# A dynamic convolution fused with a max-out layer: another order for the opening's steps, and a last copy split over two engines

## The chip, the core and the metric

The kernel runs on one core of a Trainium2 chip. The metric is the device time of one execution in microseconds. Five engines work side by side, each through its own list of instructions in order: TensorE (PE, matrix products; PEld is its weight load), VectorE (DVE), ScalarE (ACT), GpSimd (POOL) and SyncE (SP, here only an issuer of transfers). Transfers issued by SP form one queue ("hardware" in the profile), those issued by POOL another ("software"); both are moved by the same 16 DMA engines. Engines wait for each other and for transfers through semaphores.

## The reference, cut to what matters

```python
# x: (8, 4160, 192), weight_gen: (8, 4160, 8 heads, 7 taps), all float32
w = exp(weight_gen - max); w = w / w.sum(taps)        # softmax over the 7 taps
out = sum over k of w[..., h, k] * x[s - 6 + k, h*24:(h+1)*24]   # causal, zero before the sequence
x2 = out.reshape(33280, 192)
h1 = x2 @ w1; h2 = x2 @ w2                            # 192 -> 1024
return maximum(h1, h2) @ w_out                        # 1024 -> 192
```

## The kernel before, in words

The 33280 rows lie as 128 partitions of 260 columns; a column is one row of 192 numbers in each partition. Columns are handled in batches of 16 (`BATCHES`), each in two units of 8, in the first two batches in four units of 4. For a batch the softmax is worked out on ACT and DVE: exp (`exp_sum`, L153), sum over taps on DVE (`red`, L168), logarithm on ACT (`ln`, L172), subtraction on DVE (`shift`, L177), and a second exp that writes normalised weights in bfloat16 (`weights`, L191). DVE multiplies them with the seven shifted copies of x (`mul`, L211). From batch 2 on DVE also adds the seven products and a DMA transposes the sum; in the first two batches PE adds and transposes with an identity (`sum_transpose`, L281) and ACT copies the result out of PSUM (`sums_out`, L293).

The maximum is written as max(h1, h2) = h1 + relu(h2 - h1). So PE computes the hidden tile x2 @ (w2 - w1) (`hid_tile`, L336), ACT applies relu (L346), and PE adds rows of x2 @ (w1 @ w_out) (`out_first`, L388) and relu(...) @ w_out (`out_hidden`, L376) into an output bank, in a first half (`out_first`) and a second half (`out_second`); between them ACT relays a semaphore (`relay`). ACT copies the bank to SBUF (`evac`, L434) and SP stores it.

The work up to hidden tile 15 is the opening, the rest is a loop over groups of three tiles that the change does not touch. In the opening the order is written out by hand: the string `OPENING` is a list of steps, and as each step is run its instructions are appended to the lists of their engines. So the string sets the order on every engine at once. `step@other` makes a transfer wait until `other` is done. The steps, with their numbers:

- `lg.b` loads weight_gen of batch b (SP for b < 2, POOL after that). `xf` loads the first columns of x by SP, `lx.b.o.n` n columns of batch b from column o by POOL, which turns them into bfloat16 on the way. `xa`, `xv` convert the first columns on ACT and DVE.
- `lw.h.i` loads 512 columns (half h) of rows 0 to 127 of w1 (i = 0) or w2 (i = 1); `lt.h.i` the same half of the last 64 rows, into 64 partitions. All by SP. `lo` loads w_out by POOL.
- `X`, `n`, `l`, `s`, `W.b.o`: the five softmax steps. X.0, n.0, l.0 and s.0 come in halves (`.0.0.2`, `.0.1.2`). `m.b.o` is the product, `y.u` the sum on PE of unit u, `e.u` its copy on ACT (unit 0 in two halves, y.0.0 and y.0.1).
- `c.i` casts a piece of w1 (L622, ACT); `d.i` is w2 - w1 on DVE (L597); `t.i` exchanges its partition halves on PE, `T.i` copies that back on ACT (L614, L616).
- `v`, `V`: w1 transposed on PE and copied on ACT; `p`: w1 @ w_out on PE, `C.i` its three copies on ACT (L665, L667). `lh` copies the six columns that two batches share.
- `h.t`, `r.t`: hidden tile t on PE and its relu on ACT. `A.g`, `B.g`, `D.g`, `E.g`: first half, relay, second half and copy of output group g.
- `k.n` issues n matmuls on the identity that nobody reads.

Hidden tiles of the opening lie in two PSUM buffers, so h.8 can start only when r.6 has read tile 6. `evac` treats the last pair of columns apart (L422 to L425).

Of the kernel before, what the change touches and what calls it, by code (L numbers as in the profile page):

```python
# [17 lines left out]
def _sub(base: bass.AP, off: int, dims):  # L18
    ap = [list(base.ap[0])] + [[int(s), int(c)] for s, c in dims]
    return dataclasses.replace(base, offset=base.offset + off, ap=ap)  # L20
# [3 lines left out]
def kernel(  # L24
# [9 lines left out]
    nc = tc.nc  # L34

    B, S, D = x.shape
# [17 lines left out]
    def dcol(c):  # L54

        return (c + ROT) % CPP
# [292 lines left out]
    def column(c):  # L349

        for u, (b, o, n) in enumerate(UNITS):
            k = c - BATCHES[b][0] - o
            if 0 <= k < n:
                return u, k // 2, k % 2

    def place(p):

        u, i, _ = column(2 * p)
        b, o, n = UNITS[u]
        return BATCHES[b][0] + o + i, n // 2  # L360
# [55 lines left out]
    def evac(p, n):  # L416

        tile_, at = op_at[p]
        o = o_t[0]
        if p == NT // 2 - 1:  # L420

            nc.scalar.copy(out=_sub(o_last, 0, [[D, 2], [1, D]]),  # L422
                           in_=_sub(tile_, at, [[512, 2], [1, D]]))
            for j, eng in enumerate((nc.scalar, nc.sync)):
                eng.dma_start(  # L425
                    out=bass.AP(tensor=out.tensor, offset=dcol(place(p)[0] + 2 * j) * D, ap=[[CPP * D, P], [1, D]]),
                    in_=o_last[:, j * D:(j + 1) * D],
                )
            return
        runs = [[q for q in range(p, p + n) if column(2 * q)[0] == u]  # L430
                for u in range(column(2 * p)[0], column(2 * (p + n - 1))[0] + 1)]
        for qs in runs:
            c, h = place(qs[0])
            copied = nc.scalar.copy(out=_sub(o, c % 24 * D, [[D, len(qs)], [h * D, 2], [1, D]]),  # L434
                           in_=_sub(tile_, at + (qs[0] - p) * D, [[D, len(qs)], [512, 2], [1, D]]))
        stores = []
        for q in range(p, p + n):
            u, i, _ = column(2 * q)
            if u == NU - 2 and UNITS[u][2] == 8 and i % 2:
                stores.append((nc.sync, place(q)[0] - 1, [4 * D, 2], [1, 2 * D]))  # L440
            elif u < NU - 1 and i == UNITS[u][2] // 2 - 1:
                w = i + 1
                for k in range(0, 2 * w, w if u in PARTED else 2 * w):
                    stores.append((nc.sync, place(q)[0] - i + k, [1, (w if u in PARTED else 2 * w) * D]))
            if u == NU - 1:
                stores.append((nc.sync, place(q)[0], [2 * D, 2], [1, D]))
        for eng, c, *ap in stores:

            def issue(eng=eng, c=c, ap=ap, o=o):
                eng.dma_start(  # L450
                    out=bass.AP(tensor=out.tensor, offset=dcol(c) * D, ap=[[CPP * D, P], *ap]),
                    in_=_sub(o, c % 24 * D, ap),
                )

            if 3 <= u < NU - 3:
                held.append(issue)
            else:
                while u > 3 and held:
                    held.pop(0)()
                issue()  # L460
        return copied
# [8 lines left out]
    OUTS, c = [[], [], []], 0  # L470
    for g in range(3, len(GROUPS)):
        most = 4 if g == 3 else 2 if GROUPS[g][1] == 2 or len(OUTS[-1]) == 4 else 4
        n = min(most, ready[g] - c)
# [21 lines left out]
    def hidden(g, now=(), between=lambda: None, beside=lambda: None, ahead=lambda: None,  # L495
               before=lambda: None, after=lambda: None):


        t0, n = GROUPS[g]
        rd = room(g)  # L500
        for t in range(t0, t0 + n - 1):
            hid_tile(t)
        if now:
            out_room(now, "a" if n == 1 and "a" in ps else None)
            last = out_first(now)
        for t in range(t0, t0 + n - 1):
            relu(rd, t, 1)
        go = relay(last) if now else None
        hid_tile(t0 + n - 1)
        before()  # L510
        if len(now) > 2:
            beside()
        relu(rd, t0 + n - 1, 1)
        ahead()
        if now:
            out_second(now, go)
            evac(now[0] // 2, len(now) // 2)
        between()
        after()
        if len(now) <= 2:  # L520
            beside()

    def rest_of_results(c):

        parts = [p for p in (c[:4], c[4:-2], c[-2:]) if p]
        assert max(map(len, parts)) <= 4
        go = []
        for i, now in enumerate(parts):
            out_room(now, ("r", "a", "c")[i])
            go.append(relay(out_first(now)))  # L530
            if i:
                out_second(parts[i - 1], go[i - 1])
                evac(parts[i - 1][0] // 2, len(parts[i - 1]) // 2)
        out_second(parts[-1], go[-1])
        evac(parts[-1][0] // 2, len(parts[-1]) // 2)
# [10 lines left out]
    o_last = consts.tile([P, 2 * D], FP32, name="o_last")  # L546
# [155 lines left out]
    def results_buffer(_):  # L702
# [16 lines left out]
    }  # L719

    OPENING = """
        lg.0 xf.-6.6 xf.0.4 lt.1.0 lt.0.0 k.2 lw.0.1 k.19 lw.0.0 lt.1.1 lw.1.0 lt.0.1 X.0.0.2 k.1 n.0.0.2
        X.0.1.2 lw.1.1 k.1 k.2 n.0.1.2 l.0.0.2 s.0.0.2 xa.-6.4 l.0.1.2 W.0.0.0 lx.0.4.4@l.0.0.2 lg.1 xv.-2.6
        W.0.0.1 s.0.1.2 W.0.12 c.0 lx.0.12.4@W.0.12 W.0.8 m.0.0.0 m.0.0.1 W.0.4 y.0.0 y.0.1 c.2 e.0.0 c.1
        e.0.1 d.0 d.2 t.0 k.3 t.2 T.3 d.1 T.4 h.0 h.1 t.1 X.1 r.0 lx.0.8.4 T.1 lo.0 r.1 m.0.4 n.1 v.0 h.2
        lx.1.0.8 V.1 y.1 r.2 l.1 h.3 e.1 m.0.8 lg.2@l.1 s.1 V.0 m.0.12 r.3 h.4 W.1.0 m.1.0 y.2 h.5 r.4 p.0
        e.2 r.5 h.6 lx.1.8.8@r.4 lg.3@e.2 y.3 W.1.8 h.7 lh.2 C.1 C.0 C.2 A.3 W.1.4 X.2 r.6 e.3 B.3 m.1.4 h.8
        D.3 y.4 r.7 r.8 Z.0 E.3 n.2 X.3 l.2 m.1.8 A.4 e.4 W.1.12 lx.2.0.8.0@r.7 B.4 h.9 D.4 h.10 r.9 E.4 s.2
        r.10 lg.4@r.9 y.5 W.2.0 A.5 h.11 B.5 h.12 e.5 D.5 n.3 r.11 r.12 A.6 m.1.12 E.5 h.13 B.6 D.6 y.6 r.13
        E.6 h.14 e.6 l.3 lx.2.8.8@r.13 h.15 r.14 A.7 W.2.8 B.7 y.7 D.7 r.15 e.7 E.7  # L730
    """

    make_identity(nc, ident_f)
# [91 lines left out]
```

## Time and profile before

| | us |
|---|---|
| median of three runs | 405.75 (405.36 to 405.82) |
| profiled execution | 405.37 |
| span of its core | 403.6 |
| PE busy | 394.8 |
| DVE busy | 369.1 |
| ACT busy | 360.9 |
| POOL busy | 72.3 |

The span runs from the first to the last recorded instruction; 1.77 us of the profiled execution lie around it. Times in the views count from the span's start. A row of the timeline gives start, duration, engine, line, operation, tiles and count, and in brackets the idle time before it with what ended it; rows of the same kind that follow each other are merged. The granted clock of TensorE was 1.0 throughout.

### The profile page before, as it was taken

The numbers are of one execution on the slowest core, as the hardware profiler recorded it, in microseconds if no ns is written. First come the engines' busy times: TensorE is split into PE (matmuls) and PEld (weight loads), VectorE is DVE, ScalarE is ACT, GpSimd is POOL, SyncE is SP. The second block draws the span as 40 slices with busy tenths as digits, with TensorE's granted clock in tenths as the row PEclk, the third lists the DMA queues.
The fourth block names the chain that finished last, engine by engine and source line by source line (L and its number), as shares of the span: only waits on it lengthen the run. The fifth ranks groups of instructions, "written<-read, shape, count | busy, mean of one in ns | idle before, by whom it ended". The sixth has DMA issues, their size and how long they took to land.

```text
span 403.6 us, 16321 instructions
## 1 busy us (share of the span) xinstructions
PE 394.8 (98%) x7499; PEld 321.3 (80%) x7499; DVE 369.1 (91%) x211; ACT 360.9 (89%) x466; POOL 72.3 (18%) x96
## 2 busy tenths in 40 slices
PE   7799999999999999999999999999999999999996
PEld 3589999777778777778777778877777877787996
DVE  5999999999999999999999999999999999998200
ACT  5999899999999989999899999989999899888872
POOL 3111031211122210222220122122012121200000
PEclk9999999999999999999999999999999999999999
DMA  8956468767768646864766667777457847558304
GB/s 262 222 140 151 120 124 167 183 164 133 190 110 222 182 79 129 240 187 80 217 187 107 141 192 193 99 215 198 81 115 228 178 80 200 141 106 193 104 31 169
DMA packets 60883, 63.16 MB, mean 157 GB/s; under 512 B 47641, under 2 KB 48665, under 8 KB 60816
## 3 DMA queue, kind: packets, MB, share of 16 engines
q1 hardware_dynamic: 52816, 40.15, 36.4%
q0 software_dynamic: 7856, 21.89, 27.4%
q8 instruction: 58, 0.95, 1.0%
q10 hardware_dynamic: 144, 0.10, 0.1%
q14 instruction: 9, 0.07, 0.1%
HBM read 36.55 MB, written 25.56 MB: 154 GB/s over the span
## 4 chain that ended last, share of the span: by engine, by line
PE 92%; ACT 5%; DMA 1%; SPq 1%; issue 0%
PE op_ps L376 42%; PE hdc L336 13%; PE hdb L336 13%; PE hda L336 13%; PE op_ps L388 8%; ACT rd_t L346 2%; DMA ws0E<-in_moe_w_dram 1%; PE hdp L336 1%; PE yps L281 1%; ACT en_t L191 1%; ACT yt L293 1%; ACT e_t L153 0%; ACT w1t L644 0%; SPq L574 0%; ACT w L622 0%
## 5 line engine op out<-in xcount | busy, mean ns | idle before, releaser
L376 PE MATMUL op_ps<-wo,rd_t 64*128 64x192 bf16 x4160 | 210.6, 243 | 0.0
L376 PEld LDWEIGHTS <-rd_t 64*128 64x128 bf16 x4160 | 181.0, 94 | 14.7
L211 DVE TENSOR_TENSOR m_t<-xb,en_t 128x10752 bf16<-128x10752 bf16 (+2 forms) x39 | 187.8, 4821 | 1.5 <-ACT en_t L191 1.4
L336 PEld LDWEIGHTS <-wd 64*128 64x128 bf16 x1824 | 96.8, 94 | 40.4 <-issue 2.5
L346 ACT ACTIVATE rd_t<-hdc 128x1024 bf16<-128x1024 f32 x82 | 84.1, 1025 | 17.8 <-PE hdc L336 16.2
L253 POOL CAST gate<-yt 128x1 f32<-128x1 bf16 x30 | 39.9, 1332 | 271.3 <-DMA yt<-y_t 271.3
L346 ACT ACTIVATE rd_t<-hda 128x1024 bf16<-128x1024 f32 x81 | 83.4, 1030 | 0.2 <-ACT o_t L434 0.2
L346 ACT ACTIVATE rd_t<-hdb 128x1024 bf16<-128x1024 f32 x81 | 83.5, 1031 | 0.0
L227 DVE TENSOR_TENSOR m_t<-m_t 128x4608 bf16<-128x4608 bf16 (+1 forms) x30 | 73.0, 2433 | 0.1
L336 PE MATMUL hdc<-yt,wd 64*128 64x512 bf16 (+1 forms) x552 | 67.9, 353 | 0.0
L434 ACT COPY o_t<-op_ps 128x384 f32<-128x384 f32 (+1 forms) x99 | 56.1, 577 | 12.4 <-PE op_ps L376 12.3
L336 PE MATMUL hdb<-yt,wd 64*128 64x512 bf16 (+1 forms) x540 | 67.1, 355 | 0.0
L336 PE MATMUL hda<-yt,wd 64*128 64x512 bf16 (+1 forms) x540 | 67.1, 355 | 0.0
L388 PE MATMUL op_ps<-w,yt 64*128 64x192 bf16 x780 | 55.5, 243 | 0.0
L388 PEld LDWEIGHTS <-yt 64*128 64x128 bf16 x780 | 39.0, 94 | 14.5 <-issue 0.3
L233 DVE TENSOR_TENSOR m_t<-m_t 128x3072 bf16<-128x3072 bf16 (+1 forms) x30 | 50.2, 1674 | 0.1
L191 ACT ACTIVATE en_t<-wg_t 128x896 bf16<-128x896 f32 (+3 forms) x48 | 35.7, 773 | 3.0 <-PE op_ps L376 2.0
L236 DVE TENSOR_TENSOR y_t<-m_t 128x1536 bf16<-128x1536 bf16 (+1 forms) x30 | 27.5, 916 | 0.6
L177 DVE TENSOR_TENSOR wg_t<-wg_t,sum_t 128x280 f32<-128x280 f32 (+6 forms) x46 | 22.2, 483 | 0.0
L168 DVE TENSOR_REDUCE sum_t<-e_t 128x64 f32<-128x448 f32 (+3 forms) x31 | 19.7, 639 | 2.3 <-ACT e_t L153 2.3
L125 POOL DMA_DIRECT2D xb<-in_x_dram x34 | 18.2, 537 | 17.3 <-ACT rd_t L346 11.0
L153 ACT ACTIVATE e_t<-wg_t 128x896 f32<-128x896 f32 (+2 forms) x18 | 15.9, 886 | 2.1 <-DMA wg_t<-in_weight_gen_dram 2.1
(40 smaller groups left out, 110.0 us busy)
## 6 DMA issues: line engine op xcount, KB each, us to landing
out_dram<-o_t SPq DMA_DIRECT2D x21, 768.0 KB, 4.3
xb<-in_x_dram POOLq DMA_DIRECT2D x30, 384.0 KB, 5.0
out_dram<-o_t SPq DMA_DIRECT2D x22, 384.0 KB, 3.7
wg_t<-in_weight_gen_dram POOLq DMA_DIRECT2D x13, 448.0 KB, 5.7
xb<-xb POOLq DMA_DIRECT2D x7, 288.0 KB, 5.1
wg_t<-in_weight_gen_dram SPq DMA_DIRECT2D x2, 448.0 KB, 5.2
xb<-in_x_dram POOLq DMA_DIRECT2D x4, 192.0 KB, 6.4
xs<-in_x_dram SPq DMA_DIRECT2D x1, 576.0 KB, 4.3
```

The costliest lines, as they stand in the source:

```text
L177: nc.vector.tensor_tensor(out=w_t, in0=w_t, in1=_sub(s_ts[b], hs.start, [[1, hs.stop - hs.start], [0, K]]), op=ALU.subtract)
L191: act = nc.scalar.activation(out=_sub(en_ts[b], (o * WGC + ((i or 0) * J + j) * N * K) * 2, [[2 * N, K], [2, N], [1, 2]]), in_=_sub(wg_ts[ ...
L211: return nc.vector.tensor_tensor(out=m_out, in0=x_in, in1=_sub(en_ts[b], at * H * 2, [[2, K * n * H], [0, G // 2], [1, 2]]), op=ALU.mult,)
L227: nc.vector.tensor_tensor(out=taps(0, 1, 3), in0=taps(0, 1, 3), in1=taps(3, 1, 3), op=ALU.add)
L233: nc.vector.tensor_tensor(out=taps(0, 2, 2), in0=taps(0, 2, 2), in1=taps(1, 5, 2), op=ALU.add)
L236: nc.vector.tensor_tensor(out=_sub(y_ts[b], o * D, [[64, 2], [P, 3 * w // 2], [1, 64]]), in0=taps(0, 1, 1), in1=taps(2, 1, 1), op=ALU.add,)
L253: nc.gpsimd.tensor_copy(out=gate, in_=yt[:, 0:1])
L336: nc.tensor.matmul(hid_out(t, f, j), lhsT=wd_at(j, s, f // 4, f % 4 * P, P), rhs=_sub(yt_ts[u][half(j), :], (s + j) % 3 * P, [[3 * P, w // ...
L346: relu_of[t0] = nc.scalar.activation(out=rd[:, k * 1024:(k + n) * 1024], in_=hd[:, at:at + n * 1024], func=AF.Relu)
L376: return nc.tensor.matmul(op_out(c), lhsT=rd[rows, k * 1024 + at:k * 1024 + at + P], rhs=wo[rows, f * D:(f + 1) * D], start=False, stop=(r ...
L388: nc.tensor.matmul(op_out(c + j), lhsT=yt_ts[u][half(j), (3 * i + (s + j) % 3) * P:(3 * i + (s + j) % 3 + 1) * P], rhs=w10[half(j), s * D: ...
L434: copied = nc.scalar.copy(out=_sub(o, c % 24 * D, [[D, len(qs)], [h * D, 2], [1, D]]), in_=_sub(tile_, at + (qs[0] - p) * D, [[D, len(qs)] ...
```

## The change

Nothing is computed differently. The string `OPENING` is written anew, and the last evacuation is split.

- SP: the 64-row pieces and the 128-row halves of the weights are issued in turn (before: two 64-row pieces, two halves, then in turn). Number and sizes are the same.
- POOL: lx.0.4.4 is released by X.0.0.2 (before: l.0.0.2), lx.0.12.4 by W.0.0.1 (before: W.0.12); lx.1.0.8 follows at once; lx.0.8.4 now waits for e.0.0, lg.2 follows it (before: after l.1), and lo waits for m.0.4 (before: it followed lx.0.8.4 at once). lx.1.8.8 waits for W.1.4 (before: r.4), lg.3 for r.4 (before: e.2).
- ACT: W.0.4, W.0.8 and W.0.12 stand ahead of the casts c.0, c.2, c.1, and these ahead of e.0.0; the two V copies behind r.2 and r.3 (before: ahead of them), l.1 ahead of r.2; W.1.4 behind W.1.0; r.6 ahead of X.2 (before: W.1.4 and X.2 stood between C and r.6); W.1.12 behind B.4, E.6 ahead of r.13, W.2.8 at the end.
- DVE: s.0.0 ahead of n.0.1; m.1.12 ahead of n.3.
- PE: k.3 ahead of y.0.0 (before: between t.0 and t.2); t.1 ahead of h.1; y.3 ahead of h.6; h.11 and h.12 ahead of A.5, A.6 ahead of D.5.
- The last copy of two columns: ACT copies one, DVE the other (before: ACT both), each with its own store.

```diff
         if p == NT // 2 - 1:
-            nc.scalar.copy(out=_sub(o_last, 0, [[D, 2], [1, D]]),
-                           in_=_sub(tile_, at, [[512, 2], [1, D]]))
-            for j, eng in enumerate((nc.scalar, nc.sync)):
+            for j, (eng, copy) in enumerate(((nc.scalar, nc.scalar.copy), (nc.sync, nc.vector.tensor_copy))):
+                copy(out=o_last[:, j * D:(j + 1) * D], in_=tile_[:, at + 512 * j:at + 512 * j + D])
                 eng.dma_start(
...
     OPENING = """
-        lg.0 xf.-6.6 xf.0.4 lt.1.0 lt.0.0 k.2 lw.0.1 k.19 lw.0.0 lt.1.1 lw.1.0 lt.0.1 X.0.0.2 k.1 n.0.0.2
-        X.0.1.2 lw.1.1 k.1 k.2 n.0.1.2 l.0.0.2 s.0.0.2 xa.-6.4 l.0.1.2 W.0.0.0 lx.0.4.4@l.0.0.2 lg.1 xv.-2.6
-        W.0.0.1 s.0.1.2 W.0.12 c.0 lx.0.12.4@W.0.12 W.0.8 m.0.0.0 m.0.0.1 W.0.4 y.0.0 y.0.1 c.2 e.0.0 c.1
-        e.0.1 d.0 d.2 t.0 k.3 t.2 T.3 d.1 T.4 h.0 h.1 t.1 X.1 r.0 lx.0.8.4 T.1 lo.0 r.1 m.0.4 n.1 v.0 h.2
-        lx.1.0.8 V.1 y.1 r.2 l.1 h.3 e.1 m.0.8 lg.2@l.1 s.1 V.0 m.0.12 r.3 h.4 W.1.0 m.1.0 y.2 h.5 r.4 p.0
-        e.2 r.5 h.6 lx.1.8.8@r.4 lg.3@e.2 y.3 W.1.8 h.7 lh.2 C.1 C.0 C.2 A.3 W.1.4 X.2 r.6 e.3 B.3 m.1.4 h.8
-        D.3 y.4 r.7 r.8 Z.0 E.3 n.2 X.3 l.2 m.1.8 A.4 e.4 W.1.12 lx.2.0.8.0@r.7 B.4 h.9 D.4 h.10 r.9 E.4 s.2
-        r.10 lg.4@r.9 y.5 W.2.0 A.5 h.11 B.5 h.12 e.5 D.5 n.3 r.11 r.12 A.6 m.1.12 E.5 h.13 B.6 D.6 y.6 r.13
-        E.6 h.14 e.6 l.3 lx.2.8.8@r.13 h.15 r.14 A.7 W.2.8 B.7 y.7 D.7 r.15 e.7 E.7
+        lg.0 xf.-6.6 k.1 xf.0.4 lt.0.1 lw.0.1 lt.1.0 lw.0.0 k.19 X.0.0.2 n.0.0.2 lt.0.0 X.0.1.2 k.1 lw.1.0
+        k.2 lt.1.1 lw.1.1 l.0.0.2 s.0.0.2 xa.-6.4 W.0.0.0 lx.0.4.4@X.0.0.2 lg.1 k.2 W.0.0.1 n.0.1.2 xv.-2.6
+        l.0.1.2 s.0.1.2 W.0.4 lx.0.12.4@W.0.0.1 k.3 m.0.0.0 W.0.8 y.0.0 W.0.12 m.0.0.1 c.0 c.2 y.0.1 d.0 c.1
+        e.0.0 d.2 t.0 t.2 e.0.1 T.3 d.1 lx.1.0.8 T.4 h.0 t.1 X.1 r.0 h.1 lx.0.8.4@e.0.0 T.1 h.2 v.0 m.0.4
+        y.1 n.1 r.1 lg.2 h.3 l.1 lo.0@m.0.4 r.2 V.0 e.1 r.3 m.0.8 V.1 h.4 s.1 m.0.12 W.1.0 m.1.0 W.1.4 y.2
+        h.5 e.2 p.0 y.3 r.4 r.5 h.6 W.1.8 C.1 h.7 lx.1.8.8@W.1.4 C.2 lg.3@r.4 C.0 lh.2 r.6 A.3 X.2 e.3 B.3
+        m.1.4 h.8 D.3 n.2 m.1.8 y.4 r.7 r.8 Z.0 E.3 X.3 l.2 A.4 e.4 lx.2.0.8.0@r.7 B.4 h.9 D.4 h.10 W.1.12
+        r.9 s.2 m.1.12 E.4 lg.4@W.1.12 y.5 r.10 h.11 W.2.0 h.12 A.5 e.5 n.3 r.11 B.5 A.6 r.12 B.6 D.5 D.6
+        E.5 h.13 y.6 E.6 A.7 r.13 e.6 l.3 h.14 lx.2.8.8@e.6 h.15 B.7 y.7 D.7 r.14 r.15 e.7 E.7 W.2.8
     """
```

## The prediction, made before the result was known

> **What bounds the kernel.** I read the page first, then the chain that ended last, in order of time.
>
> ```profile
> span 403.6 us, 16321 instructions
> PE 92%; ACT 5%; DMA 1%; SPq 1%; issue 0%
> ```
>
> ```profile
> 3.98 5.95 DMA ws0E<-in_moe_w_dram
> ...
> 29.36 0.83 PE hdp L336 x12
> ...
> 31.51 1.22 PE yps L281 x84
> ...
> 398.04 1.99 PE op_ps L376 x48
> ```
>
> From 29.36 us to the last matrix product the chain is PE alone. The change adds no product, so what lies behind 30 us moves as a block. Only two places can change the time: the opening, by the moment at which PE stops waiting, and the tail behind 398.04 + 1.99 us. A sum on PE (y) costs 1.22 us; a hidden tile, by the start of what follows it below, 0.65, and two 1.3.
>
> Next the timeline of ACT and of PE before 30 us.
>
> ```profile
> 10.48 1.29 ACT L191 ACTIVATE en_t<-wg_t 128x224 bf16<-128x224 f32 x4
> ...
> 13.45 1.08 ACT L614 CAST wd<-turned 128x512 bf16<-128x512 f32 x2
> 14.54 0.95 ACT L153 ACTIVATE e_t<-wg_t 128x896 f32<-128x896 f32 x1
> ...
> 25.68 0.31 ACT L667 CAST w<-pw 64x192 bf16<-64x192 f32 x1
> ...
> 26.72 0.70 ACT L191 ACTIVATE en_t<-wg_t 128x224 bf16<-128x224 f32 x2
> 27.33 0.93 ACT L153 ACTIVATE e_t<-wg_t 128x896 f32<-128x896 f32 x1
> ```
>
> ```profile
> 26.99 0.41 PE L388 MATMUL op_ps<-w,yt 64*128 64x192 bf16 x6
> ...
> 27.90 0.41 PE L388 MATMUL op_ps<-w,yt 64*128 64x192 bf16 x6
> ...
> 29.36 0.83 PE L336 MATMUL hdp<-yt,wd 64*128 64x256 bf16 x12 [0.39 <-ACT rd_t L346]
> 30.01 0.33 PE L376 MATMUL op_ps<-wo,rd_t 64*128 64x192 bf16 x3
> ```
>
> ACT goes from one instruction to the next without a gap: T.3 and T.4 (13.45), X.1 (14.54), the C copies (25.68), W.1.4 (26.72), X.2 (27.33), and r.6 behind it. PE does A.3 from 26.99, two halves of 0.91 us, is done at 28.81 and then waits for r.6 with h.8, which starts at 29.36; D.3 follows at 30.01. Handover is therefore set by ACT's amount of work ahead of r.6, and that work starts at X.1.
>
> Third, DVE and the loads, since they feed both.
>
> ```profile
> 11.93 0.69 DVE L597 TENSOR_TENSOR wd<-ws1T,ws0T 128x512 bf16<-128x512 f32 x1 [0.19 <-DMA ws1T<-in_moe_w_dram]
> 13.16 0.69 DVE L597 TENSOR_TENSOR wd<-ws1E,ws0E 128x512 bf16<-128x512 f32 x1 [0.54 <-DMA ws1E<-in_moe_w_dram]
> 13.77 2.96 DVE L211 TENSOR_TENSOR m_t<-xb,en_t 128x5376 bf16<-128x5376 bf16 x1
> ...
> 17.63 2.95 DVE L211 TENSOR_TENSOR m_t<-xb,en_t 128x5376 bf16<-128x5376 bf16 x1
> ...
> 21.50 5.83 DVE L211 TENSOR_TENSOR m_t<-xb,en_t 128x5376 bf16<-128x5376 bf16 x2
> ```
>
> ```profile
> 4.97 0.58 SPq L566 DMA_DIRECT2D ws0E<-in_moe_w_dram  x1
> ...
> 5.94 0.71 POOL L125 DMA_DIRECT2D xb<-in_x_dram  x1 [3.64 <-ACT sum_t L172]
> 7.43 0.37 SPq L118 DMA_DIRECT2D wg_t<-in_weight_gen_dram  x1
> ```
>
> Issue to landing, in order: the two ws0E, lg.1, lx.0.4.4, lx.0.8.4 (issued 9.8), wo (10.3), and the later lx.1.8.8 (23.8) and lg.2 (19.9).
>
> ```profile
> DMA to landing us min/median/max: 6.0/6.3/6.6
> ```
>
> ```profile
> wg_t<-in_weight_gen_dram SPq DMA_DIRECT2D x1, 448.0 KB, 7.1
> ```
>
> ```profile
> xb<-in_x_dram POOLq DMA_DIRECT2D x1, 192.0 KB, 6.9
> ```
>
> ```profile
> xb<-in_x_dram POOLq DMA_DIRECT2D x1, 192.0 KB, 7.2
> ```
>
> ```profile
> wo<-in_moe_w_out_dram POOLq DMA_DIRECT2D x1, 384.0 KB, 8.5
> ```
>
> ```profile
> xb<-in_x_dram POOLq DMA_DIRECT2D x1, 384.0 KB, 4.6
> ```
>
> ```profile
> wg_t<-in_weight_gen_dram POOLq DMA_DIRECT2D x1, 448.0 KB, 3.5
> ```
>
> So lw.1.0 lands at 11.6 (4.97 + 6.6), the last 64-row piece, for which d.2 waited, at 11.9, lx.0.4.4 at 12.85, lg.1 at 14.53: X.1 starts just as lg.1 lands. This is the limit to be beaten, and the string's new order of ACT does not touch it.
>
> **The change part by part.**
>
> *Weights in turn.* The first ws0E stays the seventh transfer with the same bytes ahead, so it lands at 9.93 (3.98 + 5.95) and c.0 starts there as before. ACT fills its wait with W.0.4, W.0.8, W.0.12, so the four W (1.29 us) behind c.0 go; c.2 ends near 11.1. But then c.1 needs lw.1.0. That gain is cut short by the transfer, not by ACT.
>
> *lx.0.4.4 earlier.*
>
> ```profile
> 4.11 1.04 ACT L153 ACTIVATE e_t<-wg_t 128x448 f32<-128x448 f32 x2 [2.09 <-DMA wg_t<-in_weight_gen_dram]
> ```
>
> Issued at 5.94 before; released by X.0.0, the first half of this 1.04 us, it is issued near 5.0 (POOL's reaction estimated at 0.3), beside lw.1.0 and ahead of the last 64-row piece. The queues serve roughly in order of issue: issued at 5.94, it moved nothing while the hardware queue had work ahead of it; in the window 9 to 10 the list of queues has the hardware queue alone, in 10 to 11 the software queue too (packets, MB, share of 16 engines).
>
> ```profile
> q1 hardware_dynamic: 131, 0.24, 105.2%
> ```
>
> ```profile
> q0 software_dynamic: 75, 0.12, 63.2%
> ```
>
> It took 0.95 us of landing order (11.9 to 12.85). So lw.1.0 lands between 11.6 and 12.55, I take 12.0; the last 64-row piece between 11.9 and 12.85, I take 12.6, near the top, since it is now issued behind. Then d.2 ends at 13.3, t.2 and T.3 follow 0.55 later, T.4 ends near 14.85: X.1 starts at 14.85, +0.3 (bounds: 0, by lg.1, and +0.55). c.1, e.0.0 and e.0.1 run between 12.0 and d.2's end and t.2, and are hidden.
>
> *ACT from X.1 to A.3.* The same instructions, plus W.1.4, which moves ahead of the C copies: 0.61 us (26.72 to 27.33). X.2 (0.95) moves behind r.6, so r.6 is no longer what h.8 waits for; A.3's wait for C takes its place. A.3: 26.99 + 0.3 + 0.61 = 27.9, its end 29.72, h.8 0.65, D.3 at 30.37 against 30.01: **+0.36**. Without the 0.3 it would be +0.06: the two moves on ACT cancel.
>
> *DVE beside it.* d.1 ends at 14.0, m.0.4 starts 0.15 late, m.0.8 wants to start at 17.8. Its columns come by lx.0.8.4, now released by e.0.0, issued near 13.4, behind lx.0.12.4 and lx.1.0.8 (576 KB). Landing: 18.0 by the row of 4.6 us, 20.6 by its own of 7.2; I take 18.0, as the wo transfer is no longer among those ahead and they are issued some 2 us earlier. m.0.12, the first of the two products in the row of 21.50 (2.9 us each, to 24.4), then ends 0.4 late, at 24.85. On PE y.3 now stands ahead of h.6: y.3, h.6 and h.7 from 24.85 are done at 27.4, inside ACT's 27.9 for A.3. The cover is 0.5 us; each us beyond costs a us.
>
> *wo.*
>
> ```profile
> 23.02 1.49 PE L658 MATMUL pw<-wo,w1t 128*128 128x192 bf16 x16
> ```
>
> lo is issued near 17.1 (m.0.4) behind lx.0.8.4 and lg.2. Landing 20.6 (3.5 us) to 25.6 (8.5); I take 22.3, for two transfers ahead. p.0, which needs it, ran at 23.02, is wanted at 23.3 (0.3 later, as ACT) and may slip to about 23.9 before y.3, h.6 and h.7 behind it hold A.3 up. Cost nil. lx.1.8.8 and lg.3 are issued within half a us of their old times: nil.
>
> *k.3 ahead of y.0.0.*
>
> ```profile
> 11.19 0.79 PE L281 MATMUL yps<-around,m_t 64*128 64x64 bf16 x42 [0.68 <-DVE m_t L211]
> 12.14 0.81 PE L674 MATMUL warm<-around 128*128 128x512 bf16 x3
> ```
>
> At most 0.81 us later for y.0.0, which is done before 11.19 all the same, where y.0.1 waits for DVE: nil. t.1, h.11, h.12, A.6, r.13 and E.6 change places while PE is busy throughout: nil, and at most one hidden tile, 0.65, if one of them waits for its bank.
>
> *Tail.*
>
> ```profile
> 400.05 0.48 ACT L422 COPY o_last<-op_ps 128x384 f32<-128x384 f32 x1
> ```
>
> Half the columns on ACT cost 0.31 (the 64x192 row above), so the stores start **0.17** earlier; bounds 0 and 0.24 (half of 0.48). For DVE's copy no row reads PSUM. [...]
>
> **Sum** on the profiled execution: 405.37 + 0.36 - 0.17 = 405.56. The median lies 0.38 above that execution, so the forecast is 405.9 us. A difference under 0.2% (0.8 us) is about what a measurement of this kernel cannot tell from no change.
>
> **Rivals.**
>
> *The alternation speeds the loads (faster).*
>
> ```profile
> 6.00:7.00 1.00, 1.00 (x7) 0.43 (x5) 0.50 (x2) 1.00 (x5) 0.65 (x1) 1.00 1.18 246
> ...
> 8.00:9.00 1.00, 1.00 (x6) 0.49 (x5) 1.00 (x2) 0.70 (x2) 0.00 (x0) 1.00 1.08 369
> ```
>
> The columns end with the DMA share and GB/s. The two 64-row pieces issued together move while the rate is 246 GB/s; where halves move it is 369. If alternated pieces went at 369, 0.5 MB would save 0.7 us, lg.1 would land at 13.8 and X.1 start at 14.2: D.3 at 29.73, with less on DVE too 29.46. With the tail that is -0.45 to -0.72: 405.3 to 405.0. Against it: each engine still has the same packets to move. Over 0.2% needs something more that I do not see.
>
> *lx.0.8.4 is late (slower).* Landing at 19.6, the middle of its later half, m.0.8 ends at 22.6, y.3 starts at 26.5, A.3 at 29.0, D.3 at 31.5: +1.3 with the tail, 407.1. It decides from a landing of 18.5, and is over 0.2% from 19.1. The row of 7.2 us speaks for it, the shorter backlog against.
>
> *The queues share (slower).* If POOL's two loads issued at 7.6 and 8.1 take turns with lg.1 instead of following it, lg.1 lands about 1 us later, X.1 starts at 15.5, D.3 at 31.0: 406.6. The rows of 9 to 11 us speak against. [...]
>
> *wo is late (slower).* At 25.6, p.0, y.3, h.6, h.7 and A.3 follow in line, D.3 at 32.1: 407.7. It decides from 23.9.
>
> **How the numbers follow.** Forecast (opening +0.36 or near it) 0.42, alternation 0.25, lx.0.8.4 late 0.17, sharing 0.09, wo late 0.07. About half of the alternation's chance, 0.12, I put beyond -0.2%, for stalls that vanish with it. So faster 0.12, same 0.42 + 0.13 = 0.55, slower 0.33. The range 404.9 to 407.1 takes in the forecast, nearly all of the alternation, sharing, and half of lx.0.8.4: 0.42 + 0.24 + 0.09 + 0.08 = 0.83. The forecast alone: 405.5 to 406.4.
>
> **What would show it.** In the changed profile: X.1 on ACT near 14.85, bound by T.4 and not by lg.1; c.1 waiting for ws0E; lx.0.8.4 landing near 18; A.3 starting right behind the last C copy near 27.9; h.8 right behind A.3 without a wait for r.6; the copies of o_last near 0.31 instead of 0.48. It is wrong if m.0.8 waits for xb past 18.5, if p.0 waits for wo, or if lg.1 lands clearly before 14.2 or after 15.

## The result, and the profile after

The changed kernel takes 410.39 us (median of 4 runs, 410.05 to 410.97), the kernel before beside it 405.57 (405.36 to 405.82). The ratio is 1.0117, 95% interval 1.0103 to 1.0130: 4.8 us slower, outside the forecast's range of 404.9 to 407.1. The profiled execution took 410.72 us, its span is 408.9, 5.3 more than before.

The chain of work that ended last, changed kernel (start, us, what):

```profile
2.12 5.82 DMA ws1T<-in_moe_w_dram
...
7.96 10.47 DMA wg_t<-in_weight_gen_dram
...
18.45 0.95 ACT e_t L153
...
22.95 2.11 PE yps L281 x84
...
25.09 0.80 ACT yt L293
```

lg.1, the load of weight_gen for batch 1, is now on the path: issued at 7.96, landed 10.47 us later. Before it took 7.1, from 7.43. X.1 (L153) waits for it. PE waits behind X.1: the tile after its hole is h.2 (20.36), which needs the buffer that r.0 frees, and r.0 follows X.1 on ACT. ACT's and PE's timelines, changed kernel:

```profile
18.45 0.95 ACT L153 ACTIVATE e_t<-wg_t 128x896 f32<-128x896 f32 x1 [3.21 <-DMA wg_t<-in_weight_gen_dram]
```

```profile
16.27 0.83 PE L336 MATMUL hdp<-yt,wd 64*128 64x256 bf16 x12
20.36 0.29 PE L336 MATMUL hdp<-yt,wd 64*128 64x256 bf16 x2 [3.26 <-ACT rd_t L346]
...
21.58 1.37 PE L638 MATMUL tp<-around,w 128*128 128x128 bf16 x16
22.75 2.30 PE L281 MATMUL yps<-around,m_t 64*128 64x64 bf16 x84
...
33.00 0.42 PE L388 MATMUL op_ps<-w,yt 64*128 64x192 bf16 x6 [0.28 <-ACT w L664]
...
34.81 0.83 PE L336 MATMUL hdp<-yt,wd 64*128 64x256 bf16 x12
35.46 0.76 PE L376 MATMUL op_ps<-wo,rd_t 64*128 64x192 bf16 x14
```

X.1 starts 3.91 us later than before (14.54). D.3 starts at 35.46 against 30.01, 5.45 later; the other 1.54 us arise between the two. The sum y.1 takes 2.30 us where it took 1.39, the transposes of w1 1.37 where they took 0.84. Kernel before:

```profile
16.11 0.84 PE L639 MATMUL tp<-around,w 128*128 128x128 bf16 x16
...
17.51 1.39 PE L281 MATMUL yps<-around,m_t 64*128 64x64 bf16 x84
```

Stretches of PE in the changed kernel (length, busy time and count, granted clock, DMA share, GB/s) tell why:

```profile
20.00:22.00 2.00, 1.45 (x17) 0.83 0.98 103
22.00:24.00 2.00, 2.00 (x62) 0.50 0.82 96
24.00:26.00 2.00, 1.77 (x60) 0.81 0.05 11
```

After a hole of 3.26 us the clock granted to TensorE fell to one half (0.50 in 22 to 24 us), for about 3.4 us (an estimate from the three means: 0.17, 0.50 and 0.19 of 2 us each make 1.7 us lost, at a loss of one half). Behind D.3 nothing more is lost: from there to the end of the span it is 373.4 us against 373.6. The tail, changed kernel:

```profile
405.48 0.32 ACT L423 COPY o_last<-op_ps 128x192 f32<-128x192 f32 x1
...
405.83 0.36 DVE L423 COPY o_last<-op_ps 128x192 f32<-128x192 f32 x1 [24.14 <-ACT o_last L423]
406.22 0.34 SPq L424 DMA_DIRECT2D out_dram<-o_last  x1
```

DVE's copy waits for ACT's. The last store is issued 0.74 us behind the first copy's start, where it was 0.51 (400.05 to 400.56). Kernel before:

```profile
400.56 0.34 SPq L425 DMA_DIRECT2D out_dram<-o_last  x1
```

Why lg.1 is late shows in its neighbours. POOL's pair of issues before and after, and the list of queues (packets, MB, share of 16 engines) in the windows 12 to 13, 13 to 14 and 16 to 17 us of the changed kernel:

```profile
9.25 1.07 POOL L125 DMA_DIRECT2D xb<-in_x_dram  x2 [2.60 <-ACT en_t L191]
```

```profile
7.65 1.07 POOL L125 DMA_DIRECT2D xb<-in_x_dram  x2 [1.81 <-ACT sum_t L172]
```

```profile
q1 hardware_dynamic: 93, 0.20, 60.7%
q0 software_dynamic: 65, 0.09, 50.5%
...
q0 software_dynamic: 66, 0.10, 55.3%
q1 hardware_dynamic: 65, 0.20, 53.4%
...
q0 software_dynamic: 103, 0.17, 98.4%
q1 hardware_dynamic: 6, 0.01, 5.9%
```

In 12 to 14 us SP's queue (q1) and POOL's (q0) share the DMA engines about half and half (60.7 and 50.5%, then 53.4 and 55.3%), and at the end lg.1's last packets trickle through (5.9% in 16 to 17 us) beside a queue that takes nearly everything (98.4%). Two edits meet there. The early releases put lx.0.12.4 and lx.1.0.8 into POOL's queue at 7.65 and 8.18 (before: lx.0.12.4 at 9.25, and lx.0.8.4 second, at 9.77). And lg.1's issue on SP waits until SP's fourth transfer, the first 64-row piece of the weights, has landed (the chain above): at 7.94, where it was 7.41 before. What runs beside that piece is now a 128-row half and no second 64-row piece. So lg.1 went from 1.8 us ahead of POOL's pair into the midst of it.

### The profile page after: what moved, and what is told of

It is laid out like the page before. It is cut to its first block, busy times and chain, and to the rows that moved or that the text cites. A ratio compares the mean times of both kernels' runs of the same rounds, so it can differ in the third digit from the quotient of the medians.

```text
span 408.9 us, 16320 instructions
## 1 busy us (share of the span) xinstructions
PE 397.5 (97%) x7499; PEld 321.6 (79%) x7499; DVE 369.9 (90%) x212; ACT 361.1 (88%) x466; POOL 70.5 (17%) x96
## 4 chain that ended last, share of the span: by engine, by line
PE 92%; DMA 4%; ACT 3%; SPq 0%; issue 0%; DVE 0%
PE op_ps L376 42%; PE hdc L336 13%; PE hdb L336 13%; PE hda L336 13%; PE op_ps L388 8%; DMA wg_t<-in_weight_gen_dram 3%; PE yps L281 2%; PE hdp L336 1%; DMA ws1T<-in_moe_w_dram 1%; ACT rd_t L346 1%; ACT en_t L191 0%; ACT yt L293 0%; PE tp L638 0%; ACT e_t L153 0%; SPq L557 0%; ACT w1t L643 0%
## 5 line engine op out<-in xcount | busy, mean ns | idle before, releaser
L253 POOL CAST gate<-yt 128x1 f32<-128x1 bf16 x30 | 38.1, 1270 | 270.9 <-DMA yt<-y_t 270.9
L125 POOL DMA_DIRECT2D xb<-in_x_dram x34 | 18.2, 536 | 30.5 <-ACT sum_t L172 10.5
```

The source lines that it names most:

```text
L253: nc.gpsimd.tensor_copy(out=gate, in_=yt[:, 0:1])
```

## The experiments

Times are compared with the kernel before, measured on the same chip in the same series. Run-to-run scatter is wider in the variants than in the two kernels, so each reading rests on a profile.

**Undoing or doing one of the two edits on the loads.** Four runs: the changed kernel with lx.1.0.8 late (`a_lx1late`), the kernel before with the early releases (`b_lxearly`), the kernel before with the alternated weights (`b_alt`), the changed kernel with the old order of weights (`a_oldw`).

```diff
 a_lx1late:  - d.1 lx.1.0.8 T.4 ... lx.0.8.4@e.0.0 T.1 h.2     + d.1 T.4 ... lx.0.8.4@e.0.0 T.1 lx.1.0.8 h.2
 b_lxearly:  - lx.0.4.4@l.0.0.2 ... lx.0.12.4@W.0.12 (lx.1.0.8 after h.2)
             + lx.0.4.4@X.0.0.2 ... lx.0.12.4@W.0.0.1 lx.1.0.8
 b_alt:      - lt.1.0 lt.0.0 k.2 lw.0.1 k.19 lw.0.0 lt.1.1 lw.1.0 lt.0.1
             + lt.0.1 lw.0.1 k.2 lt.1.0 k.19 lw.0.0 lt.0.0 lw.1.0 lt.1.1
 a_oldw:     - lt.0.1 lw.0.1 lt.1.0 lw.0.0 k.19 ... lt.0.0 ... lt.1.1
             + lt.1.0 lt.0.0 lw.0.1 lw.0.0 k.19 ... lt.1.1 ... lt.0.1
```

> The changed kernel with one step moved: lx.1.0.8 (384 KB by POOL) is issued behind lx.0.8.4, as in the order before, and not ahead of it. Theory Q (POOL's early loads take DMA time from lg.1): lg.1 lands near 15 to 15.5 instead of 18.4, X.1 waits at most 0.5 us for it, PE has no hole over 1.5 us before h.2 and its clock stays at 1.0, time 406.3 to 407.3. Theory W (the alternated weights delay lg.1, by their own pace and by the semaphore that lg.1's issue waits for): lg.1 still lands near 18, time about 410.

> The kernel before with POOL's early releases alone: lx.0.4.4 released by X.0.0, lx.0.12.4 by W.0.0.1, lx.1.0.8 right behind it. Weights, ACT, DVE and tail as before. Theory Q: lg.1, issued at 7.4, lands at 16.5 to 18.4 instead of 14.5, X.1 waits 2 to 4 us, time 408 to 410. Theory W: lg.1 within 0.7 us of 14.5, time 405.4 to 406.3.

> The kernel before with the alternated order of the weights alone on SP. Theory Q: the first ws0E lands near 10.5 (9.93 before), lg.1 is issued 0.5 us later and lands near 15, X.1 0.5 us later, time 406.0 to 406.4. Theory W: lg.1 lands at 17 to 18.4, time 408 to 410.

> The changed kernel with the weights in the order of before on SP, all else as changed. Theory Q: lg.1 is issued at 7.4 again but still shares with POOL's loads: lands at 16.5 to 18.4, time 408.5 to 410. Theory W: lg.1 near 14.5 to 15, time 406 to 406.7.

Measured, against 405.75: 409.91, 406.72, 406.74 and 407.16 us. Neither theory holds alone. Each edit by itself costs 1.0 us in the medians (X.1 at 15.32 and 15.27); in the rows D.3 comes 0.79 and 0.69 us late (30.80 and 30.70), and the interval of `b_alt`, 0.9999 to 1.0056 of the kernel before, just reaches no change. With the old weights the changed kernel loses 1.4 of its 4.8 us. X.1 starts at 15.67 there.

In `a_lx1late` lg.1 lands early too (X.1 at 15.87), and yet the time hardly moves. PE there stands still twice with no releaser at all:

```profile
25.39 0.29 PE L281 MATMUL yps<-around,m_t 64*128 64x64 bf16 x8 [1.57 <-issue]
...
31.32 1.05 PE L336 MATMUL hdp<-yt,wd 64*128 64x256 bf16 x16 [1.78 <-issue]
```

This is a second mechanism, which no theory so far had.

**Both edits on the loads, in the old order of the engines** (`b_both`: `b_alt` and `b_lxearly` together).

> The kernel before with two parts of the change and no other: the weights alternated, and lx.0.4.4, lx.0.12.4 and lx.1.0.8 released early. Each alone put X.1 at 15.3 us and cost 1.0 us. Theory L (the two together let POOL's loads overtake lg.1, whatever the order on the engines): lg.1 is issued after lx.0.12.4 and lands at 17.5 to 18.6, X.1 starts with it, PE stands idle for over 2.5 us around 17 to 20, and the time is 409 to 411, as much as the whole change. Rival A (the prices add): lg.1 lands at 15.8 to 16.2 and the time is 407.2 to 408. Rival O (the reordered steps of ACT, DVE and PE are needed for the loss): 406.5 to 407.5.

408.59 us (two runs) against 405.47. X.1 at 17.14, the changed order not needed:

```profile
16.93 0.84 PE L639 MATMUL tp<-around,w 128*128 128x128 bf16 x16
19.05 0.29 PE L336 MATMUL hdp<-yt,wd 64*128 64x256 bf16 x2 [1.28 <-ACT rd_t L346]
```

The loads alone cost 3.1 of the 4.8 us, over the range that adding the prices gave (407.2 to 408) and under the 409 to 411 that I expected. The rows show why no more: X.1 is 1.31 us sooner than in the changed kernel, the old order has the transposes of w1 (tp) ahead of h.2, where they fill part of the hole (1.28 us are left), and the mean granted clock stays at 1.000 in this execution (0.995 in the other run). The new order has them behind h.2.

**lg.1 ahead of POOL's pair, all else as changed** (`a_lg1`: lx.0.12.4 released by W.0.4; `a_lg2`: by c.0).

```diff
- W.0.0.1 ... W.0.4 lx.0.12.4@W.0.0.1 k.3 m.0.0.0 W.0.8 y.0.0 W.0.12 m.0.0.1 c.0 c.2
+ W.0.0.1 ... W.0.4 lx.0.12.4@W.0.4 k.3 m.0.0.0 W.0.8 y.0.0 W.0.12 m.0.0.1 c.0 c.2        (a_lg1)
+ W.0.0.1 ... W.0.4 k.3 m.0.0.0 W.0.8 y.0.0 W.0.12 m.0.0.1 c.0 lx.0.12.4@c.0 c.2          (a_lg2)
```

> The changed kernel with one trigger put back: lx.0.12.4, and so lx.1.0.8 behind it on POOL, wait for W.0.4 (the copy of weights that runs first) instead of W.0.0.1, which puts their issue near 9.3 and 9.8 us, behind lg.1's at 8.0. The alternated weights stay. Theory L: lg.1 lands late because it is issued in the midst of POOL's two loads (7.65 and 8.18 us); issued ahead of both it lands at 15.2 to 15.9, X.1 follows at once, PE's hole ahead of h.1 is at most 1 us, the granted clock stays at 1.00, and the time is 406.3 to 407.5. Rival W2: the alternated weights alone keep the queue full until 18 us whatever POOL does; lg.1 lands at 17.5 or later and the time stays at 409 to 411. Third: lg.1 early, but PE pauses with nothing to wait for as in the run with lx.1.0.8 alone moved (1.57 and 1.78 us); then 408 to 410.

> The changed kernel with lx.0.12.4, and lx.1.0.8 behind it, released by c.0, the first cast of w1 (near 11 us), 3 us behind lg.1's issue; the release by W.0.4 gave lg.1 only 0.34 and 0.88 us of lead and it still landed at 17.86. Alternated weights and the order of the engines stay. Theory L: lg.1 lands at 14.8 to 15.8, PE's hole ahead of h.1 is under 1 us, the granted clock stays at 1.00. Theory F (PE's instructions): with the hole gone PE runs into pauses that have no releaser, behind a late instruction load, as in the runs with lx.1.0.8 or the old loads (0.7 to 3.9 us in all); so 407 to 410 and not 405.8. Rival W2: alternation alone delays lg.1, which lands at 17 or later, and the time is 409.5 to 411.

W.0.4 is done sooner than I had thought: in `a_lg1` the pair went out at 8.40 and 8.94, 0.34 and 0.88 us behind lg.1 (8.06), which landed at 17.86; 410.17 us. (In that series the kernel before scattered from 405.3 to 411.0, so its times tell nothing under 1%.) In `a_lg2` the pair followed at 11.66, and lg.1, issued at 8.11, landed at 14.74, though the weights were alternated. So with the alternated weights lateness is set by how soon POOL's loads follow, and alternation alone does not make it. Nor does the place of lg.1 among POOL's issues: with the old weights it is issued behind lx.0.12.4 in `a_oldw` too (7.67 after 7.61) and between POOL's loads in `b_fetch` below (8.61; 8.27 and 9.09), and it lands 8.0 and 7.7 us after its issue, not 10.5. Why the alternated order makes the sharing so much dearer no run here shows.

`a_lg2` took 407.44 us (406.89 to 410.36) against 405.47. X.1 started at 15.08 right behind T.4, as forecast, there is no hole ahead of h.2, and in the profiled execution (408.83 us) most of what was lost was lost to two pauses:

```profile
24.86 0.29 PE L281 MATMUL yps<-around,m_t 64*128 64x64 bf16 x8 [1.62 <-issue]
...
30.23 1.05 PE L336 MATMUL hdp<-yt,wd 64*128 64x256 bf16 x16 [1.23 <-issue]
```

The list of queues of `a_lg2`, windows 21 to 22.5 and 22.5 to 23.6:

```profile
q0 software_dynamic: 617, 0.23, 129.7%
...
q8 instruction: 1, 0.02, 5.5%
```

Queue 8 loads instructions, 16,384 bytes at a time (all 58 packets in the trace of the kernel before); this packet ran from 22.56 to 23.52, as soon as POOL's backlog was through, and PE went on at 24.86. The next ran from 27.84 to 28.74, and PE went on at 30.23. From one pause to the next PE runs 128 products in `a_lg2` (8, 12, 16, 84 and 8 in the rows from 24.86 to 28.40 us) and 128 in `a_lx1late` (the same rows from 25.39 to 28.94). The page of the kernel before counts as many weight loads as products on PE, 7499 of each; at one weight load a product the 128 are 256 instructions. That these packets are PE's is read from this and from that page: both counts together beside 58 packets are 259 a packet.

**What delays PE's instructions.** `b_act` is the kernel before with the changed order on ACT, DVE and PE, the old order of loads and the old tail; only lx.0.12.4 has another trigger than before, W.0.4 in place of W.0.12. `b_fetch` differs from it in one transfer.

```diff
- y.1 n.1 r.1 h.3 l.1 lg.2@l.1 r.2 V.0 e.1 r.3 m.0.8 V.1 h.4
+ y.1 n.1 r.1 h.3 l.1 r.2 V.0 e.1 r.3 m.0.8 V.1 lg.2@V.1 h.4
```

> The kernel before with the changed kernel's order of steps on ACT, DVE and PE in the opening (casts of w1 ahead, relus and copies reordered), but with the old order of the weights, the old triggers and order of POOL's loads, and the old tail. Prediction's step: the reorderings cancel; X.1 within 0.4 us of 14.54, A.3 at 26.8 to 27.6, time 405.3 to 406.3. Rival O: the order itself makes the kernel late (casts of w1 ahead of other work, r.1 behind v.0): A.3 at 28 or later and 406.6 or more.

> The run with the old loads and the changed order of the engines, with one load moved: lg.2 is released by V.1 (near 23.5 us) instead of l.1 (19.7). In that run PE paused for 1.24 us in y.2 with no releaser, and went on 1.46 us after the instruction queue's transfer of 22.80 to 23.70 had landed, while POOL's queue was taking 77 to 79% of the DMA engines with lg.2. Theory F1 (that transfer comes late because it stands behind lg.2's packets): with lg.2 away it runs by 22.5 and the pause in y.2 is gone or under 0.5 us. Theory F2 (it is asked for only when PE comes to a place in its program, and takes 2.4 us from there however idle the DMA engines are): the pause stays at 1.0 to 1.5 us. The time itself may go either way, since later transfers move too: 406.5 to 411.

`b_act` took 410.97 us (408.68 to 412.44), a miss: the moved W steps release POOL's second load at 8.51 already, lg.1 is issued at 7.97, X.1 starts at 15.97, and PE pauses for 1.24, 0.49 and 2.18 us (in the profiled execution, the slowest of four). `b_fetch` took 409.47 (two runs). The same sum in `b_act` and in `b_fetch`:

```profile
25.16 0.29 PE L281 MATMUL yps<-around,m_t 64*128 64x64 bf16 x8 [1.24 <-issue]
```

```profile
18.22 0.28 PE L336 MATMUL hdp<-yt,wd 64*128 64x256 bf16 x2 [1.17 <-ACT rd_t L346]
...
22.97 1.40 PE L281 MATMUL yps<-around,m_t 64*128 64x64 bf16 x84
...
29.39 0.42 PE L388 MATMUL op_ps<-w,yt 64*128 64x192 bf16 x6 [0.29 <-ACT w L665]
```

With lg.2 out of the way the instruction packet ran at 21.45 instead of 22.80 and this pause is gone: in `b_act` the packet of queue 8 came late because POOL's stood in its way (75.4% of the engines in 21 to 22.8 us there, no packet of POOL in `b_fetch`). `b_fetch` pauses later all the same, for 0.59 us at 41.66 and 0.41 at 49.39; what delays PE there was not shown. The first and the last row, h.2 and A.3, are used below. Why the old order of the engines shows none in `b_alt`, `b_lxearly` and `b_both` is argued, not shown: there PE waits 0.82 us for e.1 ahead of h.4, just when its second packet is on the way (19.21 to 20.19 and a wait until 20.38 in the kernel before). The old order is not free of them: `b_cancel` below pauses for 1.51 us at 48.22.

**The clock.** Fifteen products on the identity that nobody reads, behind h.1 (`a_warm`) and between t.1 and h.1 (`a_warm2`).

```diff
- T.4 h.0 t.1 X.1 r.0 h.1 lx.0.8.4@e.0.0
+ T.4 h.0 t.1 X.1 r.0 h.1 k.15 lx.0.8.4@e.0.0        (a_warm)
+ T.4 h.0 t.1 k.15 X.1 r.0 h.1 lx.0.8.4@e.0.0        (a_warm2)
```

> The changed kernel with 15 products of keep_warm behind h.1, where PE stood idle for 3.26 us. lg.1 still lands near 18.4. Theory C (the clock is a term of its own): the granted clock stays at 1.00 between 20 and 26 us, the sums y.1 take 1.4 us instead of 2.30 and the transposes 0.85 instead of 1.37, A.3 starts 1.2 to 1.5 us earlier (31.5 to 31.8) and the time is 408.7 to 409.4. Rival: the slow stretch lies beside work of ACT and DVE that is as late anyway; y.1 is quick but A.3 stays at 32.7 to 33.1, and the time at 410.0 to 410.8.

> The changed kernel with 15 products of keep_warm between t.1 and h.1, that is in the 3.26 us in which PE stood idle; in the run that had them behind h.1 they came after that hole, ran on the slow clock for 4.70 us and made it worse. lg.1 still lands near 18. Theory C: the granted clock stays at 1.00 from 20 to 26 us, y.1 takes 1.4 us instead of 2.30, the transposes 0.85 instead of 1.37, A.3 starts 1.2 to 1.6 us earlier than 33.0 and the time is 408.6 to 409.4. Rival: A.3 within 0.3 us of 33.0 and 410.0 to 410.8, since ACT and DVE are as late anyway. Theory F adds: PE comes early to y.2 and may pause there without a releaser, which takes part of the gain back.

Both missed in time. `a_warm` (415.46 us) had them behind the hole, where they ran slowly for 4.70 us; it differs in more than the products, since h.1, at 16.27 in the changed kernel, there waits 3.07 us for r.0 and starts at 19.76. In `a_warm2` (411.57, two runs) the clock fell before them (0.70 in 16 to 18 us), behind an idle 2.12 us at 12.6 and short waits after it. PE in `a_warm2`, and its stretches:

```profile
17.39 4.81 PE L673 MATMUL warm<-around 128*128 128x512 bf16 x15
22.13 1.48 PE L336 MATMUL hdp<-yt,wd 64*128 64x256 bf16 x24
23.55 0.85 PE L638 MATMUL tp<-around,w 128*128 128x128 bf16 x16
24.23 1.40 PE L281 MATMUL yps<-around,m_t 64*128 64x64 bf16 x84
...
33.64 0.42 PE L388 MATMUL op_ps<-w,yt 64*128 64x192 bf16 x6 [0.29 <-ACT w L664]
```

```profile
18.00:20.00 2.00, 2.00 (x7) 0.50 0.70 240
20.00:22.00 2.00, 2.00 (x10) 0.94 0.48 37
22.00:24.00 2.00, 2.00 (x33) 1.00 1.36 162
```

The products delay h.1 to 22.13. But from h.1 on the clock is whole, and y.1 takes 1.40 and the transposes 0.85. What the low clock costs on the way to A.3 is read from `b_fetch`, which has the changed order of the engines, a whole clock (1.00 from 14 to 34 us; y.1 takes 1.40 us and the transposes 0.85) and no pause before D.3: there A.3 follows 11.17 us behind h.2 (18.22 to 29.39), in the changed kernel 12.64 (20.36 to 33.00). So the low clock is worth about 1.5 us between h.2 and A.3. `a_warm2` does not recover it, since the filling costs more.

**The order on ACT and the tail, without the loads.**

```diff
 b_cancel:  - C.1 C.0 C.2 A.3 W.1.4 X.2 r.6      + W.1.4 C.1 C.0 C.2 A.3 r.6 X.2
 b_r6:      - A.3 W.1.4 X.2 r.6                  + A.3 W.1.4 r.6 X.2
 b_tail:    the last copy as in the change
 b_split:   b_tail, with the last column's products in a PSUM tile of their own:
            + o_b.append(ps["b"].tile([P, 1024], FP32, name="op_ps2", tag="b"))   # and op_out(NT - 1) in it
            + o_lasts = [consts.tile([P, D], FP32, name=f"o_last{j}") for j in range(2)]   # one for each copy to write
 b_best:    b_split and b_r6, and     - r.2 l.1 h.3 e.1      + r.2 e.1 l.1 h.3
```

> The kernel before with the last copy shared by ACT and DVE as in the change, nothing else. Prediction's step: 0.17 us faster, DVE's copy beside ACT's. Theory T, from the changed kernel's last rows (ACT's copy at 405.48, DVE's at 405.83 behind it, store issued 0.74 us behind the first copy's start instead of 0.51): the two copies of one PSUM tile run one behind the other, the last store is issued 0.2 to 0.25 us later and the time is 0.1 to 0.4 us longer (405.8 to 406.1), which the times may not resolve; the rows will.

> The kernel before with the last copy shared by ACT and DVE as in the change, but with the last column's products in a PSUM tile of their own, so that the two copies read two tiles. Theory T2 (the two copies ran one behind the other because they read one tile): DVE's copy starts within 0.1 us of ACT's, both take 0.3 to 0.4 us, the last store is issued 0.32 to 0.40 us behind the first copy's start instead of 0.51, and the time is 0.1 to 0.2 us shorter, less than the times may resolve. Rival: DVE's copy still starts when ACT's is done, last store 0.7 us behind.

> The kernel before with two moves on ACT alone: W.1.4 ahead of the C copies, r.6 ahead of X.2. Prediction's step (+0.06, the two cancel): A.3 starts 0.6 us later than in the kernel before (27.5 to 27.7), h.8 follows it without a wait, D.3 at 29.9 to 30.2, time 405.3 to 405.9. Rival: the moves bring pauses of PE without a releaser, or one of the two is not worth what the rows say; D.3 0.4 us or more away from 30.0.

> The kernel before with r.6 ahead of X.2 and nothing else. Prediction's step: A.3 stays at 27.0, h.8 follows it at 28.8 without a wait, D.3 at 29.4 to 29.5 instead of 30.0, and the time is 0.4 to 0.6 us shorter (405.0 to 405.3). Rival: X.2, 0.95 us later, delays the sums behind it, or PE pauses for its instructions since it comes to them earlier; then no gain.

> The kernel before with what the rows promise a gain for: r.6 ahead of X.2, e.1 (the cast of y.1) ahead of l.1, so that h.3 waits 0.2 us less, and the last column in a PSUM tile of its own, copied by DVE beside ACT. By rows 0.55 + 0.2 + 0.15 = 0.9 us shorter: 404.6 to 405.0, faster than both kernels. Rival: PE pauses without a releaser take it back: 405.3 or more.

`b_tail` took 407.47 us in the series in which the kernel before scattered (408.05), ratio 0.999, 0.995 to 1.003: nothing to be read from times. Its rows repeat the changed kernel's: copies at 400.15 and 400.50, last store at 400.88, 0.73 us behind. In `b_split` the copies run side by side:

```profile
400.30 0.36 DVE L425 COPY o_last<-op_ps 128x192 f32<-128x192 f32 x1 [23.76 <-PE op_ps L378]
400.33 0.32 ACT L425 COPY o_last<-op_ps 128x192 f32<-128x192 f32 x1
...
400.70 0.42 SPq L426 DMA_DIRECT2D out_dram<-o_last  x1
```

Last store 0.40 us behind the first copy, 0.11 less than before; 405.70 against 405.76 us, not to be told apart. So the order came from what the two copies shared, not from the engines. They shared the PSUM tile that they read and the SBUF tile that they write, and `b_split` parts both, so the runs do not tell which. Against the SBUF tile speaks that in the changed kernel ACT and DVE write different parts of the tile wd at once (ACT from 14.17 for 1.07 us, DVE from 14.43 for 0.69).

`b_cancel`: 405.74 against 405.76, ratio 1.0002 (0.9987 to 1.0018). A.3 at 27.56 waits 0.31 for C, h.8 follows without a wait, D.3 is at 30.03 where it was at 30.01: the two moves cancel. (The profiled execution took 407.41 us; its pause comes far behind D.3.) `b_r6`: 405.67, ratio 0.9992 (0.9977 to 1.0007). D.3 comes 0.38 us sooner, and it is gone one group later:

```profile
29.63 1.48 PE L376 MATMUL op_ps<-wo,rd_t 64*128 64x192 bf16 x32
30.95 1.48 PE L281 MATMUL yps<-around,m_t 64*128 64x64 bf16 x84
32.73 0.42 PE L388 MATMUL op_ps<-w,yt 64*128 64x192 bf16 x6 [0.29 <-ACT o_t L434]
```

A.4 waits for ACT's copy E.3, at 32.73 against 32.59 before. `b_best`: 405.47 (405.13 to 405.80), ratio 0.9985 (0.9970 to 1.0000). Its D.3 is 0.49 us sooner (29.52), and A.4 is at 32.76 again, with the same wait. It may be 0.15% faster than the kernel before; that is not certain, and much less than the 0.9 us that the rows promised. Against the changed kernel, measured in another series, it is 4.9 us shorter. (The tile that waits for e.1 is h.4, by the order of the matrix products in the kernel before, where it starts at 20.38; h.3 does not wait.)

## Why the prediction was wrong

- *"The queues serve roughly in order of issue."* This is the step that failed, and with it "X.1 starts at 14.85". It was read from the window 9 to 11 us, where POOL's first load only begins to move (first packet at 10.12 us, 4.2 us after its issue). Where both had work they shared: 66.6 and 41.1% in 11 to 12 us of the kernel before already, 53 and 55% in 13 to 14 us of the changed one. The rival "the queues share" named this, with a chance of 0.09 and 1 us for lg.1. That is about its price with the old weights (X.1 0.78 us late in `b_lxearly`, 1.13 in `a_oldw`); in the changed kernel it measured 3.91. Halves are what 12 to 14 us show; the 5.9% of 16 to 17 us no run here explains.
- *Weights in turn, "the same bytes ahead".* The second step that failed: for lg.1 the sum put the alternation at nothing. The prediction kept its issue at 7.43, ahead of POOL's pair at 7.6 and 8.1; pieces and halves in turn hold it back to 7.96, and the first ws0E, taken to land at 9.93 as before, landed at 10.56. Alone this makes X.1 0.73 us late (`b_alt`), with the early loads 2.60 (`b_both`). The slip of half a us is not the whole of it, since `a_oldw` and `b_fetch` have lg.1 in the midst of POOL's loads too and land it within 8.0 us of its issue, not 10.5; the rest of the cause stays open.
- *The clock.* No step asked what a hole in PE does to the products behind it. It is worth about 1.5 us by `b_fetch`, and the changed order helped it to happen, since it took the transposes of w1 from the hole. X.1 (3.91) and the clock (1.47) make 5.38 of the 5.45 at D.3; the rest is near the +0.06 of the two moves on ACT.
- *lx.0.8.4 at 18.0, wo at 22.3.* They landed at 19.85 and 24.72, but everything behind X.1 was late by then, and neither held anything. The two rivals about them did not come to a test.
- *"The two moves on ACT cancel", +0.06.* Right: D.3 +0.02 in `b_cancel`; in the changed profile A.3 waits for C and h.8 does not wait for r.6, as said.
- *"What lies behind 30 us moves as a block."* Right for the 5.45 us, wrong for a gain: `b_r6` gave back 0.38 at A.4.
- *Tail -0.17.* Wrong in sign: +0.23, as DVE's copy runs behind ACT's. ACT's duration was right, 0.32 (0.31 forecast); DVE's copy, for which the kernel before has no row, took 0.36.
- *"Rivals: the alternation speeds the loads."* The last 64-row piece landed at 12.98, and at 12.38 in `b_alt`, later than the 11.90 before. It did not speed anything.

## What to carry to other kernels

Ask of each transfer on the path which other queue has work from its issue to its landing: loads released 1.6 and 3.0 us sooner elsewhere, together with a new order of the transfers ahead, cost the critical one 3.9 us here. Look whether PE keeps something to do while it waits, since the late X.1 cost twice here (3.91 us, and another 1.47 by the clock behind the hole), and count a bank or a copy behind each gain before booking it. When nothing releases an engine, look at the queue that loads its instructions.

## What the runs showed that was not expected

- PE's instructions come by a DMA queue (queue 8 in the lists, counted on the same 16 engines as the data), in packets of 16,384 bytes that take about 1.0 us (median 0.99 in the kernel before, 0.97 in the changed one). PE went on 1.34 to 1.63 us after such a packet ended, in all 13 pauses without a releaser that the traces of this case hold (in `a_lx1late`, `a_oldw`, `a_lg2`, `a_warm`, `a_warm2`, `b_act`, `b_fetch` and `b_cancel`). A backlog of POOL's loads delayed one: 22.80 us in `b_act` with lg.2 ahead, 21.45 in `b_fetch` without.
- Two edits that cost 1.0 us each in the medians cost 3.1 together, with the engines' order unchanged; at X.1 it is 0.78 and 0.73 us against 2.60.
- The granted clock fell to 0.50 after a hole of 3.26 us in the changed kernel, but also in `a_lg1`, where no hole was longer than 1.98 us, with one of 1.69 before it (up to 14.48 us). So a hole of 3 us was not needed for it here. In `a_lx1late`, with pauses of 1.57 and 1.78 us, the mean clock stayed at 1.000; what sets the fall was not shown. The row of the 1.98 us and a stretch behind it, `a_lg1`:

```profile
19.80 0.29 PE L336 MATMUL hdp<-yt,wd 64*128 64x256 bf16 x2 [1.98 <-ACT rd_t L346]
```

```profile
22.00:24.00 2.00, 2.00 (x84) 0.50 1.35 161
```

- Two engines that copied different halves of one PSUM tile into different halves of one SBUF tile did not do so at once (0.35 us apart, with the second waiting for the first); with a tile of each kind of their own they started within 0.03 us.
